# Linformer attention followed by a squared-ReLU FFN: a first batch in two token chunks, a new load order, crossbar transposes of Q, and attention spread over the FFN

## The chip, the cores and the metric

One core of one Trainium2 chip. The metric is device time in microseconds (us); medians of several runs are given. Engines: PE is the matrix engine, DVE the vector engine, ACT the scalar engine, POOL and SP the two engines that issue the DMAs here. PSUM is the memory that holds the accumulators of the matmuls. The granted clock is the share of full speed that PE's clock is allowed at a time, as the profile records it. All runs used are fast (executions without the slower clock that some show).

## The reference

Eight batches of 1024 tokens, 8 heads of 64. Keys and values are first projected along the sequence to 64 rows (E and F); the result of attention is the input of an FFN with 2048 hidden units.

```python
k_proj = np.einsum('ks,bhsd->bhkd', E, k)             # E, F: 64 x 1024
v_proj = np.einsum('ks,bhsd->bhkd', F, v)
scores = q @ k_proj.transpose(0, 1, 3, 2) / 8         # then softmax over 64 columns
x = (softmax(scores) @ v_proj)                        # -> (8192 tokens, 512)
h = np.maximum(x @ w_in, 0.0)                         # w_in 512 x 2048
out = (h * h) @ w_out                                 # w_out 2048 x 512
```

## The kernel before

Attention of a batch is a list of stages; the stages of batch b+1 are put between the FFN groups of batch b. Only PE's order is fixed by the program text; a scheduler orders the other engines. Batch 0's attention has no FFN to hide behind.

```python
kvq = load(0)                       # K, V, Q of batch 0, 1 MB each in bf16, cast while loading
...                                 # w_in in 4 pieces, w_out in 4 pieces; then load(1) in the loop
    def transpose_q(self, pr):      # one head pair: 8 PE transposes of 128x128
        ps = att_psum([P, 2, TCH], BF16)
        ...
        nc.vector.tensor_copy(t[:], ps[:])
    def scores(self, pr):           # 4 matmuls, then ACT: Exp over 128x1024
    def values(self, pr):           # sums (ones), values; ACT: Ln, Exp(-x); DVE: multiply
    def stages(self):               # (stage, FFN groups to wait before it)
        yield self.project, 3
        yield lambda: self.transpose_q(0), 2
        yield self.transpose_k, 1
        for pr in range(NPAIR):
            yield lambda pr=pr: self.scores(pr), 2
            if pr + 1 < NPAIR:
                yield lambda pr=pr: self.transpose_q(pr + 1), 1
            yield lambda pr=pr: self.values(pr), 2
...
        for stage_fn, _ in cur.stages():      # batch 0: everything before its FFN
            stage_fn()
        for b in range(B):
            nxt = Attention(b + 1, load(b + 1)) if b + 1 < B else None
            ...                               # FFN groups of b with the stages of b+1 between
```

An FFN group is 4 matmuls (first layer, one of 16 blocks, then ACT ReLU and DVE square) or 16 matmuls (second layer, one of 4 token blocks, then ACT copy and a store), for each half of the tokens: 40 groups, 256 matmuls of 128x512 per batch.

The softmax here doesn't subtract the row's maximum and nothing guards it: scores larger than these inputs give would overflow.

Of the kernel before, what the change touches and what calls it, by code (L numbers as in the profile page):

```python
# [13 lines left out]
PE = mybir.EngineType.PE  # L14


@with_exitstack
def kernel(
# [18 lines left out]
    assert D == 64 and KP == 64 and C == CM == 512 and S == 1024 and H % 2 == 0  # L37
# [5 lines left out]
    TCH = NT * P  # L43
    WP = 4
    SCALE = 1.0 / float(D) ** 0.5

# [5 lines left out]
    stage = ctx.enter_context(tc.tile_pool(name="stage", bufs=2))  # L52
# [11 lines left out]
    def att_psum(shape, dtype):  # L64
        return aps.tile(shape, dtype, tag="att", name="ps_att")

    def ffn_psum():
        return fps.tile([P, 512], F32, tag="ffn", name="ps_ffn")

    def load(b):  # L70
        tiles = []
        for name, src in (("K_sb", k), ("V_sb", v), ("Q_sb", q)):
            t = qkv_pool.tile([P, H, NI * D], BF16, name=name)
            nc.gpsimd.dma_start(t[:], src[b].rearrange("h (p i) d -> p h (i d)", i=NI))
            tiles.append(t)
        return tiles
# [3 lines left out]
    for src in (E, F):  # L80
        t = stage.tile([KP, S], F32, name="e_f32")
        nc.sync.dma_start(t[:], src[:])
        e_f32.append(t)
    kvq = load(0)
    nc.scalar.preload_act_table_set("natural_log_exp_and_others")
    ident = const_pool.tile([P, P], BF16, name="ident")
    make_identity(nc, ident[:])
    ones = const_pool.tile([P, D], BF16, name="ones")
# [5 lines left out]
    fw = FF // WP  # L94
    for j in range(WP):
        t = wpool.tile([P, NCB, fw], BF16, name=f"w_in_{j}")
        nc.gpsimd.dma_start(t[:], w_in_view[:, :, j * fw:(j + 1) * fw])
        w_in_sb.append(t)
    for j in range(WP):
        n = NFB // WP  # L100
        t = wpool.tile([P, n, DM], BF16, name=f"w_out_{j}")
        nc.gpsimd.dma_start(t[:], w_out_view[:, j * n:(j + 1) * n, :])
        w_out_sb.append(t)

    def w_in_blk(cb, fb):
        n = fw // P
        return w_in_sb[fb // n][:, cb, (fb % n) * P:(fb % n + 1) * P]

    def w_out_blk(fb):
        n = NFB // WP  # L110
        return w_out_sb[fb // n][:, fb % n, :]

    projT = []
    for n, src in zip(("ET", "FT"), e_f32):
        e_bf = stage.tile([KP, S], BF16, name="e_bf")
        nc.vector.tensor_copy(e_bf[:], src[:])
        ps = att_psum([P, NI, KP], BF16)
        view = e_bf[:].rearrange("k (p i) -> k i p", i=NI)
        for i in range(NI):
            nc.tensor.transpose(ps[:, i, :], view[:, i, :], ident[0:KP, 0:KP])  # L120
        t = const_pool.tile([P, NI, KP], BF16, name=n)
        nc.vector.tensor_copy(t[:], ps[:])
        projT.append(t)
    ET, FT = projT

    class Attention:


        def __init__(self, b, kvq):
            self.K, self.V, self.Q = kvq  # L130
            self.xT = x_pool.tile([P, NCB, 2 * TCH], BF16, name="xT")
            self.exp, self.ps_x = {}, {}

        def project(self):
            ps = att_psum([P, C], F32)
            kv = self.K[:].rearrange("p h (i d) -> p h i d", i=NI)
            vv = self.V[:].rearrange("p h (i d) -> p h i d", i=NI)
            for i in range(NI):
                f, l = i == 0, i == NI - 1
                nc.tensor.matmul(ps[0:KP, :], lhsT=ET[:, i, :], rhs=kv[:, :, i, :], start=f, stop=l)  # L140
                nc.tensor.matmul(ps[KP:P, :], lhsT=FT[:, i, :], rhs=vv[:, :, i, :], start=f, stop=l)  # L141

            self.kp = proj_pool.tile([KP, H, 2, D], BF16, name="kp")
            ps_k = ps[0:KP, :].rearrange("k (h d) -> k h d", h=H)
            nc.vector.tensor_copy(self.kp[:, :, 0, :], ps_k)
            nc.vector.tensor_copy(self.kp[:, :, 1, :], ps_k)
            self.vp = proj_pool.tile([P, H, D], BF16, name="vp")
            ps_v = ps[KP:P, :].rearrange("k (h d) -> k h d", h=H)
            nc.scalar.copy(self.vp[KP:P], ps_v)
            nc.scalar.copy(self.vp[0:KP], ps_v)  # L150

        def transpose_k(self):
            ps = att_psum([P, H, KP], BF16)
# [4 lines left out]
            self.kT = proj_pool.tile([P, H, KP], BF16, name="kT")  # L158
            nc.vector.tensor_copy(self.kT[:], ps[:])

        def transpose_q(self, pr):
            ps = att_psum([P, 2, TCH], BF16)
            for a in range(2):
                for n in range(NT):
                    nc.tensor.transpose(  # L165
                        ps[:, a, n * P:(n + 1) * P], self.Q[:, 2 * pr + a, n * P:(n + 1) * P], ident[:]
                    )
            t = qt_pool.tile([P, 2, TCH], BF16, name="qT")
            nc.vector.tensor_copy(t[:], ps[:])  # L169
            self.qt = getattr(self, "qt", {})  # L170
            self.qt[pr] = t

        def qT(self, h):
            return self.qt[h // 2][:, h % 2, :]


        def scores(self, pr):
            h0, h1 = 2 * pr, 2 * pr + 1
            ps = att_psum([P, 2, TCH], F32)
            lo, hi = slice(0, 64), slice(64, 128)  # L180
            q0, q1 = self.qT(h0), self.qT(h1)

            for o, bank, h, r, qt in ((lo, 0, h0, lo, q0), (hi, 0, h0, hi, q0),
                                      (hi, 1, h1, lo, q1), (lo, 1, h1, hi, q1)):
                nc.tensor.matmul(ps[o, bank, :], lhsT=self.kT[r, h, :], rhs=qt[r], start=True, stop=True)  # L185
            e = soft_pool.tile([P, 2, TCH], BF16, name="expT")
            nc.scalar.activation(e[:], ps[:], AF.Exp, scale=SCALE)  # L187
            self.exp[pr] = e

        def values(self, pr):  # L190
            h0, h1 = 2 * pr, 2 * pr + 1
            e = self.exp.pop(pr)
            lo, hi = slice(0, 64), slice(64, 128)

            quads = ((lo, 0, h0, lo, 0), (hi, 0, h1, hi, 1), (hi, 1, h1, lo, 1), (lo, 1, h0, hi, 0))
            ps_s = att_psum([P, 2, TCH], F32)
            for o, par, h, r, bank in quads:
                nc.tensor.matmul(ps_s[o, par, :], lhsT=ones[r, :], rhs=e[r, bank, :], start=True, stop=True)  # L198
            ps_x = att_psum([P, 2, TCH], F32)
            for o, par, h, r, bank in quads:  # L200
                nc.tensor.matmul(ps_x[o, par, :], lhsT=self.vp[r, h, :], rhs=e[r, bank, :], start=True, stop=True)  # L201
            rs = soft_pool.tile([P, 2, TCH], F32, name="rs")
            nc.scalar.activation(rs[:], ps_s[:], AF.Ln)  # L203
            nc.scalar.activation(rs[:], rs[:], AF.Exp, scale=-1.0)  # L204
            nc.vector.tensor_tensor(  # L205
                out=self.xT[:, pr, :].rearrange("p (a t) -> p a t", a=2), in0=ps_x[:], in1=rs[:], op=ALU.mult
            )

        def stages(self):

            yield self.project, 3
            yield lambda: self.transpose_q(0), 2
            yield self.transpose_k, 1
            for pr in range(NPAIR):
                yield lambda pr=pr: self.scores(pr), 2
                if pr + 1 < NPAIR:
                    yield lambda pr=pr: self.transpose_q(pr + 1), 1
                yield lambda pr=pr: self.values(pr), 2

    def ffn_groups(b, xT):  # L220

        groups = []

        def first(ch, hsq, fb):
            ps = ffn_psum()
            for cb in range(NCB):
                nc.tensor.matmul(  # L227
                    ps[:], lhsT=w_in_blk(cb, fb), rhs=xT[:, cb, ch * TCH:(ch + 1) * TCH],
                    start=(cb == 0), stop=(cb == NCB - 1),
                )  # L230
            r = relu_pool.tile([P, TCH], BF16, name="h_relu")
            nc.scalar.activation(r[:], ps[:], AF.Relu)  # L232
            nc.vector.tensor_tensor(out=hsq[:, fb, :], in0=r[:], in1=r[:], op=ALU.mult)  # L233

        def second(ch, hsq, tb):
            ps = ffn_psum()
            for fb in range(NFB):
                nc.tensor.matmul(  # L238
                    ps[:], lhsT=hsq[:, fb, tb * P:(tb + 1) * P], rhs=w_out_blk(fb),
                    start=(fb == 0), stop=(fb == NFB - 1),  # L240
                )
            o = out_pool.tile([P, DM], F32, name="o_sb")
            nc.scalar.copy(o[:], ps[:])  # L243
            nc.sync.dma_start(out_rows[b, 2 * tb + ch, :, :], o[:])

        for ch in range(2):
            hsq = hsq_pool.tile([P, NFB, TCH], BF16, name="hsq")
            for fb in range(NFB):
                groups.append(lambda ch=ch, hsq=hsq, fb=fb: first(ch, hsq, fb))
            for tb in range(NT):  # L250
                groups.append(lambda ch=ch, hsq=hsq, tb=tb: second(ch, hsq, tb))
        return groups

    with tc.manual_schedule(engines={PE}):
        cur = Attention(0, kvq)
        for stage_fn, _ in cur.stages():
            stage_fn()
        for b in range(B):
            nxt = Attention(b + 1, load(b + 1)) if b + 1 < B else None
# [41 lines left out]
```

## Time and profile before

| | before |
|---|---|
| time, median | 565.35 us (565.28 with the run beside the changed kernel) |
| span of the profiled run | 563.9 us |
| first FFN matmul | 41.23 us |
| batch 1's FFN begins | 117.55 us |
| period of the later batches | 64.42 us |

From the page of the kernel before: the first line is the busy time of each engine; then the span in 40 slices of 14.1 us with the busy tenths of PE, the granted PE clock in tenths of full speed, and the DMA engines' busy tenths; the last is the chain of work that ended last, by engine.

```profile
PE 522.4 (93%) x2841; PEld 232.1 (41%) x2896; DVE 178.8 (32%) x349; ACT 284.0 (50%) x433; POOL 28.4 (5%) x38
...
PE   1565999999999999999999999999999999999996
...
PEclk9856999999999999999999999999999999999999
DMA  8999996037431736019241546010101001020201
...
PE 79%; DMA 8%; ACT 7%; DVE 4%; issue 1%; POOL 1%; ACTq 0%; POOLq 0%
```

PE is the limit everywhere but in the first four slices. There the DMA engines are full, PE is idle for a good part, and its granted clock falls to 0.5 and 0.6 in the third and fourth slice.

The PE timeline of the kernel before: start, length, engine, source line, operation, destination <- sources, count, and in brackets the idle time before it with what ended it.

```profile
22.57 0.62 PE L165 MATMUL ps_att<-ident,Q_sb 128*128 128x128 bf16 x8 [1.48 <-DMA Q_sb<-in_q_dram]
...
35.12 1.01 PE L165 MATMUL ps_att<-ident,Q_sb 128*128 128x128 bf16 x8 [1.36 <-ACT expT L187]
...
41.23 1.06 PE L227 MATMUL ps_ffn<-xT,w_in_112 128*128 128x512 bf16 x2 [0.33 <-issue]
43.95 4.00 PE L227 MATMUL ps_ffn<-xT,w_in_112 128*128 128x512 bf16 x9 [1.65 <-DVE xT L205]
47.93 0.64 PE L140 MATMUL ps_att<-K_sb,ET 128*64 128x512 bf16 x1
53.04 0.58 PE L141 MATMUL ps_att<-V_sb,FT 128*64 128x512 bf16 x1 [4.48 <-DMA V_sb<-in_v_dram]
...
117.55 2.75 PE L227 MATMUL ps_ffn<-xT,w_in_112 128*128 128x512 bf16 x12
...
134.95 0.61 PE L165 MATMUL ps_att<-ident,Q_sb 128*128 128x128 bf16 x8 [0.31 <-DVE xT L205]
...
181.97 2.75 PE L227 MATMUL ps_ffn<-xT,w_in_112 128*128 128x512 bf16 x12
...
504.08 3.62 PE L227 MATMUL ps_ffn<-xT,w_in_112 128*128 128x512 bf16 x16
```

Read three things here. Batch 0's head pairs follow one another some 4.7 us apart until 41 us, because PE waits for ACT in each (the 35.12 line). PE then stops 4.48 us for V of batch 1, which the program asks for after only three FFN groups (the 53.04 line). And in steady state a Q transpose group can wait, too (the 134.95 line). From 181.97 - 117.55 comes the period, the time from the start of one batch's FFN to the next one's, of 64.42 us. Of it 256 x 0.216 = 55.3 us are FFN matmuls, which follow each other every 0.216 us here, and the other 9.1 us are attention with the waits around it. The last line shown is the start of the last batch.

### The profile page before, as it was taken

What the parts mean: (1) busy time and instruction counts of PE and PEld (TensorE: products, weight loads), DVE (VectorE), ACT (ScalarE), POOL (GpSimd) and SP (SyncE); (2) the same over time, 40 slices, a digit from 0 to 9 for tenths busy, and PEclk for the clock granted to TensorE, in tenths of its full rate; (3) what the DMA queues carried; (4) which work ended last, traced back from release to release, by engine and by line L of the source; (5) the groups of instructions that cost most, each with busy time, mean ns of one, the idle gap of its engine ahead of it and who ended that gap; (6) DMA issues with size and microseconds to landing.
All of it is one profiled execution on the core that took longest, in us unless ns stands there. A gap on an engine that the chain in (4) does not pass through costs nothing.

```text
span 563.9 us, 7122 instructions
## 1 busy us (share of the span) xinstructions
PE 522.4 (93%) x2841; PEld 232.1 (41%) x2896; DVE 178.8 (32%) x349; ACT 284.0 (50%) x433; POOL 28.4 (5%) x38
## 2 busy tenths in 40 slices
PE   1565999999999999999999999999999999999996
PEld 0221444444444444444444444444444444444442
DVE  1231524235050532325150442415141341504030
ACT  0261747347381656438282565628383564725351
POOL 6120100010000100010000100000000000000000
PEclk9856999999999999999999999999999999999999
DMA  8999996037431736019241546010101001020201
GB/s 152 207 206 207 207 212 115 33 67 126 92 58 58 128 78 112 20 60 146 71 81 56 100 88 132 2 75 1 56 20 38 38 7 69 0 76 0 76 0 74
DMA packets 38592, 47.11 MB, mean 84 GB/s; under 512 B 1568, under 2 KB 30240, under 8 KB 38560
## 3 DMA queue, kind: packets, MB, share of 16 engines
q0 software_dynamic: 29184, 29.36, 32.8%
q1 hardware_dynamic: 9376, 17.31, 8.2%
q8 instruction: 22, 0.36, 0.3%
q14 instruction: 10, 0.08, 0.0%
HBM read 59.24 MB, written 16.78 MB: 135 GB/s over the span
## 4 chain that ended last, share of the span: by engine, by line
PE 79%; DMA 8%; ACT 7%; DVE 4%; issue 1%; POOL 1%; ACTq 0%; POOLq 0%
PE ps_ffn L238 39%; PE ps_ffn L227 32%; DMA V_sb<-in_v_dram 4%; DMA w_in_114<-in_moe_w_in_dram 4%; DVE xT L205 3%; ACT rs L204 3%; PE ps_att L165 2%; ACT rs L203 2%; PE ps_att L140 2%; ACT h_relu L232 1%; PE ps_att L198 1%; PE ps_att L185 1%; DVE hsq L233 1%; PE ps_att L141 1%; PE ps_att L201 1%
## 5 line engine op out<-in xcount | busy, mean ns | idle before, releaser
L232 ACT ACTIVATE h_relu<-ps_ffn 128x512 bf16<-128x512 f32 x256 | 147.4, 597 | 73.1 <-PE ps_ffn L227 73.0
L233 DVE TENSOR_TENSOR hsq<-h_relu 128x512 bf16<-128x512 bf16 x256 | 105.4, 423 | 216.2 <-ACT h_relu L232 215.7
L238 PEld LDWEIGHTS <-hsq 128*128 128x128 bf16 x1024 | 98.8, 98 | 120.3 <-issue 4.5
L243 ACT COPY o_sb<-ps_ffn 128x512 f32<-128x512 f32 x64 | 37.5, 586 | 173.7 <-PE ps_ffn L238 173.7
L227 PE MATMUL ps_ffn<-xT,w_in_112 128*128 128x512 bf16 x255 | 64.7, 394 | 2.0 <-DVE xT L205 1.7
L238 PE MATMUL ps_ffn<-w_out_124,hsq 128*128 128x512 bf16 x255 | 65.6, 379 | 0.1
L238 PE MATMUL ps_ffn<-w_out_120,hsq 128*128 128x512 bf16 x255 | 65.6, 380 | 0.0
L238 PE MATMUL ps_ffn<-w_out_122,hsq 128*128 128x512 bf16 x248 | 65.1, 379 | 0.4
L238 PE MATMUL ps_ffn<-w_out_126,hsq 128*128 128x512 bf16 x235 | 62.3, 379 | 1.1
L227 PE MATMUL ps_ffn<-xT,w_in_114 128*128 128x512 bf16 x241 | 59.7, 381 | 1.5 <-issue 1.1
L227 PE MATMUL ps_ffn<-xT,w_in_116 128*128 128x512 bf16 x256 | 60.3, 380 | 0.0
L227 PE MATMUL ps_ffn<-xT,w_in_118 128*128 128x512 bf16 x248 | 58.6, 379 | 1.2 <-issue 1.1
L205 DVE TENSOR_TENSOR xT<-ps_att,rs 128x1024 bf16<-128x1024 f32 x32 | 39.2, 1225 | 53.0 <-ACT rs L204 53.0
L169 DVE COPY qT<-ps_att 128x1024 bf16<-128x1024 bf16 x32 | 22.1, 692 | 67.2 <-PE ps_att L165 67.0
L227 PEld LDWEIGHTS <-w_in_112 128*128 128x128 bf16 x256 | 23.8, 100 | 37.1 <-issue 13.5
L227 PEld LDWEIGHTS <-w_in_118 128*128 128x128 bf16 x256 | 24.2, 98 | 28.5 <-issue 1.6
L227 PEld LDWEIGHTS <-w_in_116 128*128 128x128 bf16 x256 | 23.6, 98 | 29.8 <-issue 4.5
L227 PEld LDWEIGHTS <-w_in_114 128*128 128x128 bf16 x256 | 23.8, 98 | 29.0 <-issue 3.9
L203 ACT ACTIVATE rs<-ps_att 128x1024 f32<-128x1024 f32 x32 | 32.9, 1027 | 4.9 <-PE ps_att L198 4.9
L204 ACT ACTIVATE rs<-rs 128x1024 f32<-128x1024 f32 x32 | 33.8, 1056 | 1.0
L187 ACT ACTIVATE expT<-ps_att 128x1024 bf16<-128x1024 f32 x32 | 32.7, 1023 | 1.9 <-PE ps_att L185 1.9
L141 PE MATMUL ps_att<-V_sb,FT 128*64 128x512 bf16 x64 | 18.6, 443 | 8.9 <-DMA V_sb<-in_v_dram 8.9
(43 smaller groups left out, 191.3 us busy)
## 6 DMA issues: line engine op xcount, KB each, us to landing
out_dram<-o_sb SPq DMA_DIRECT2D x64, 256.0 KB, 2.0
K_sb<-in_k_dram POOLq DMA_DIRECT2D x8, 1024.0 KB, 10.5
V_sb<-in_v_dram POOLq DMA_DIRECT2D x8, 1024.0 KB, 14.6
Q_sb<-in_q_dram POOLq DMA_DIRECT2D x8, 1024.0 KB, 10.9
w_in_112<-in_moe_w_in_dram POOLq DMA_DIRECT2D x1, 512.0 KB, 20.9
w_in_114<-in_moe_w_in_dram POOLq DMA_DIRECT2D x1, 512.0 KB, 22.0
w_in_116<-in_moe_w_in_dram POOLq DMA_DIRECT2D x1, 512.0 KB, 23.5
w_in_118<-in_moe_w_in_dram POOLq DMA_DIRECT2D x1, 512.0 KB, 25.3
```

The source lines that it names most:

```text
L140: nc.tensor.matmul(ps[0:KP, :], lhsT=ET[:, i, :], rhs=kv[:, :, i, :], start=f, stop=l)
L141: nc.tensor.matmul(ps[KP:P, :], lhsT=FT[:, i, :], rhs=vv[:, :, i, :], start=f, stop=l)
L169: nc.vector.tensor_copy(t[:], ps[:])
L187: nc.scalar.activation(e[:], ps[:], AF.Exp, scale=SCALE)
L203: nc.scalar.activation(rs[:], ps_s[:], AF.Ln)
L204: nc.scalar.activation(rs[:], rs[:], AF.Exp, scale=-1.0)
L205: nc.vector.tensor_tensor(out=self.xT[:, pr, :].rearrange("p (a t) -> p a t", a=2), in0=ps_x[:], in1=rs[:], op=ALU.mult)
L227: nc.tensor.matmul(ps[:], lhsT=w_in_blk(cb, fb), rhs=xT[:, cb, ch * TCH:(ch + 1) * TCH], start=(cb == 0), stop=(cb == NCB - 1),)
L232: nc.scalar.activation(r[:], ps[:], AF.Relu)
L233: nc.vector.tensor_tensor(out=hsq[:, fb, :], in0=r[:], in1=r[:], op=ALU.mult)
L238: nc.tensor.matmul(ps[:], lhsT=hsq[:, fb, tb * P:(tb + 1) * P], rhs=w_out_blk(fb), start=(fb == 0), stop=(fb == NFB - 1),)
L243: nc.scalar.copy(o[:], ps[:])
```

## The change

Its intent: let the FFN start sooner, keep PE from waiting at the start, and take the Q transposes off PE.

1. Batch 0 goes through attention in two halves of 512 tokens. Only the first half precedes the FFN, as two groups of two head pairs; the second half's attention lies between FFN steps of the first half.
2. Loads: K, then half of Q, then V in two pieces, the weights, and the other half of Q last. In the first chunk the FFN uses them as they come: four accumulators side by side for the first four blocks, contraction block by contraction block, then two token blocks at a time through the pieces of w_out.
3. Batch 1's attention starts at step 36 of 64 of batch 0.
4. From batch 2 on Q is transposed by one transposing DMA (`dma_start_transpose`, called the crossbar below), in place of 32 PE transposes and four DVE copies.
5. The second layer is cut into steps of 4 matmuls, and attention stages stand at fixed steps. One of the two copies of the projected V moves from ACT to DVE.

```diff
-    kvq = load(0)
+    load(K0[:], tokens(k, 0))
+    load(Q0[:, :, 0:4, :], tokens(q, 0, i=slice(0, 4)))
+    for g in range(2):
+        load(V0[:, 4 * g:4 * g + 4], tokens(v, 0, h=slice(4 * g, 4 * g + 4)))
 ...                                   # w_in, w_out in four pieces each, as before
+    load(Q0[:, :, 4:8, :], tokens(q, 0, i=slice(4, 8)))
 ...
+        def keep_v(self, ps_v, h=slice(0, 8)):
+            nc.scalar.copy(self.vp[HI, h], view)
+            nc.vector.tensor_copy(self.vp[LO, h], view)
+        def transpose_q_dma(self):
+            nc.sync.dma_start_transpose(
+                self.qT[:].rearrange("p h n t -> p (h n) t"), self.Q[:].rearrange("p h i d -> p (h i d)"))
 ...
-        for stage_fn, _ in cur.stages():
-            stage_fn()
+        att.project_k()
+        for hg in range(2):
+            att.transpose_q_chunk(0, Q0, hg)
+        att.transpose_k()
+        att.chunk_scores(0, 0)
+        att.chunk_scores(0, 1)
+        att.project_v(0)
+        att.chunk_sums(0, 0)
+        att.chunk_sums(0, 1)
+        att.project_v(1)
+        att.chunk_values(0, 0)
+        att.chunk_values(0, 1)
         for b in range(B):
+            if b == 0:
+                at(19, lambda: cur.transpose_q_chunk(1, Q0, 0))   # ... second chunk at steps 19 to 29
+            if b + 1 < B:
+                t0 = 36 if b == 0 else 4
+                at(t0, nxt.project)
+                at(t0 + 3, nxt.transpose_k)
+                if b == 0:                                        # four PE transpose groups for batch 1
+                    at(t0 + 5 + gap * pr, lambda pr=pr, a=nxt: a.transpose_q(pr))
+                else:
+                    nxt.transpose_q_dma()
+                    ...
+                at(t0 + 7 + gap * pr, lambda pr=pr, a=nxt: a.scores(pr))
+                at(t0 + 10 + gap * pr, lambda pr=pr, a=nxt: a.values(pr))
```

## The prediction

> **What bounds the kernel now.** The matrix engine: the page has PE busy 93% of the 563.9 us span, and 79% of the chain that ended last is PE. The timeline shows two regimes.
>
> *Steady state, from 117.6 us on.* Batches start 64.42 us apart (117.55, 181.97, 246.39 us). FFN matmuls follow each other every 0.216 us, 256 of them 55.4 us; the other 9.07 us are attention of the next batch, of which four Q transpose groups take 4 x 0.445 us, plus a 0.31 us wait. Windows by stage show PE 98 to 99% busy at full clock: only removed PE work helps.
>
> *Start, to 117.6 us.* One batch of FFN and two of attention, 55.4 + 2 x 9 = 73.5 us of warm PE work; 44 us are lost. K lands at 12.5, V 17.5, Q 22.6 us, 5.05 us per loaded MB; the DMA engines stay full until about 83 us. The four head pairs of batch 0 pass one after another, 4.7 us each (exp 1.02, Ln 1.03, Exp 1.06 on ACT, multiply 1.23 on DVE); FFN begins at 41.2 us, really at 44. PE then waits 4.5 us for V of batch 1 (to 53). The granted clock is 0.50 to 0.73 from 20 to 60 us; matmuls then follow every 0.427 us.
>
> **What changes.**
> 1. Half of Q goes before V, all weights before batch 1. Estimated arrivals from 5.05 us per MB: K 12.5, Q half 15 to 16.5, V by 21, w_in 23 to 31, w_out by 41, other Q half 44, K and V of batch 1 48 and 53.
> 2. Only half the tokens pass attention before the FFN, as two groups instead of four pairs. Estimated chain: K projection to 16, keeps and transposes to 19.4, scores and exps to 22, two Ln, two Exp, V keeps and multiplies to 30. The FFN begins at about 28.5 us instead of 41.2, its first 4 to 5 us at half clock (2 us lost). The Trainium skill, "TensorE: Matmul & The Clock Gate", Part 1, says about 3.4 us of activity releases the throttle; this trace agrees roughly (dense from 53.0, full rate near 57.5).
> 3. The second half's attention (3.6 us of PE) and batch 1's (8.8 us) fall between FFN groups, spaced wider than their ACT chains. Batch 1 should start at 28.5 + 2 + 55.4 + 3.6 + 8.8, about 98.5 instead of 117.6: 19 us won.
> 4. For batches 2 to 7, crossbar transposes replace 32 PE transposes and four 0.69 us DVE copies each. PE saves 2.1 us per batch, six times 12.5 us. The instruction order has them nearly a batch ahead. This trace has no transpose; the skill's "DMA: Bandwidth & Descriptors", Rules for kernel authors, states 261 GB/s, so 1 MB would take 4 us (estimate from that page). Even 10 us is hidden: the output has four buffers and stores come 3.5 us apart.
> 5. Attention spread: about 0.
>
> The end (4.5 us tail) stays.
>
> **Sum.** 565.35 - 19 - 12.5 = 534 us. Range 529 to 541 us. Chances: faster by over 2% 0.96, within 2% 0.02, slower 0.02.
>
> **What would show it.** First w_in matmul near 28.5 us; no PE wait on V of batch 1; full clock from 34 us; batch 1 starting near 98.5 us; period 62.3 us afterwards; transposes landing within 10 us and no PE wait on qT; PE busy about 96%.
>
> **What would make it wrong.** Transposes of tens of us that hold the output stores behind them, so that ACT and then PE wait; shorter Q runs slowing the first loads; the PSUM pool that FFN now shares with projection and transposes making PE wait; a clock low for longer, from PE pauses in the first FFN groups.

## The result, and the profile after

| | before | after |
|---|---|---|
| time, median | 565.28 us | 529.81 us |
| ratio | | 0.9373 (95% interval 0.9346 to 0.94) |
| span | 563.9 us | 527.9 us |
| first FFN matmul | 41.23 us | 26.74 us |
| batch 1's FFN begins | 117.55 us | 95.86 us |
| period, later batches | 64.42 us | 62.09 us |

A ratio is the mean time of one kernel's fast runs over that of the other's in the same rounds, so it is not quite the ratio of the medians.

From the page of the changed kernel, the same lines:

```profile
PE 504.0 (95%) x2693; PEld 219.8 (42%) x2744; DVE 170.6 (32%) x338; ACT 286.0 (54%) x426; POOL 29.6 (6%) x40
...
PE   1699999999999999999999999999999999999996
...
PEclk9989999999999999999999999999999999999999
DMA  9999999999965554282501932100102011010102
...
PE 94%; DMA 2%; ACT 1%; issue 1%; DVE 1%; POOLq 0%
```

From the DMA view of the changed kernel, the line of the crossbar transposes (issuing queue, count, median us from issue to landing), and from the view of the tile qT their spread:

```profile
qT<-Q_sb SPq DMA_TRANSPOSE x6, 9.0
...
DMA to landing us min/median/max: 5.5/9.0/16.1
```

PE is now full from the third slice on, and 94% of the chain is PE. Its timeline:

```profile
12.15 3.57 PE L177 MATMUL ps_bank<-K_sb,ET 128*64 128x512 bf16 x8 [4.62 <-DMA K_sb<-in_k_dram]
15.66 1.54 PE L203 MATMUL ps_bank<-ident,Q_sb 128*128 128x128 bf16 x16
...
22.52 0.41 PE L238 MATMUL ps_att<-expT,vp 64*64 64x256 bf16 x8
26.17 0.41 PE L238 MATMUL ps_att<-expT,vp 64*64 64x256 bf16 x8 [3.24 <-DVE vp L163]
26.74 5.09 PE L306 MATMUL ps_bank<-xT,w_in_110 128*128 128x512 bf16 x15 [0.16 <-issue]
31.87 3.61 PE L306 MATMUL ps_bank<-xT,w_in_112 128*128 128x512 bf16 x16
...
95.86 3.69 PE L306 MATMUL ps_bank<-xT,w_in_110 128*128 128x512 bf16 x16
...
158.02 3.62 PE L306 MATMUL ps_bank<-xT,w_in_110 128*128 128x512 bf16 x15
...
220.10 3.62 PE L306 MATMUL ps_bank<-xT,w_in_110 128*128 128x512 bf16 x16
...
468.44 3.62 PE L306 MATMUL ps_bank<-xT,w_in_110 128*128 128x512 bf16 x16
```

The lines at 26.74 and 31.87 us show the clock: the first 16 matmuls of the FFN (15 are recorded) took 5.1 us, the next 16 took 3.6 us. The single records of the first 16 follow each other every 0.427 us (half speed) until 30.3 us and every 0.216 us (full speed) after it; the clock record has 0.50 from 26.93 to 30.34 us. The wait of PE before 26.17 us is new; it comes back below.

Where the 36.0 us of span came from, as differences of the batch starts:

- the start: 117.55 - 95.86 = 21.7 us;
- six periods, 386.53 us before (504.08 - 117.55) and 372.58 after (468.44 - 95.86): 13.95 us;
- the last batch with its tail: 0.4 us.

### The profile page after: what moved, and what is told of

The parts are those of the page before. It is cut to its first block, busy times and chain, and to the rows that moved or that the text cites. A ratio compares the mean times of both kernels' runs of the same rounds, so it can differ in the third digit from the quotient of the medians.

```text
span 527.9 us, 6755 instructions
## 1 busy us (share of the span) xinstructions
PE 504.0 (95%) x2693; PEld 219.8 (42%) x2744; DVE 170.6 (32%) x338; ACT 286.0 (54%) x426; POOL 29.6 (6%) x40
## 4 chain that ended last, share of the span: by engine, by line
PE 94%; DMA 2%; ACT 1%; issue 1%; DVE 1%; POOLq 0%
PE ps_bank L312 42%; PE ps_bank L306 42%; PE ps_bank L169 2%; DMA K_sb<-in_k_dram 2%; PE ps_att L228 2%; PE ps_att L234 2%; PE ps_att L238 1%; PE ps_bank L177 1%; PE ps_bank L193 0%; ACT rs L247 0%; ACT rs L248 0%; PE ps_bank L213 0%; ACT h_relu L302 0%; DVE qT L207 0%; PE ps_bank L203 0%
## 5 line engine op out<-in xcount | busy, mean ns | idle before, releaser
L302 ACT ACTIVATE h_relu<-ps_bank 128x512 bf16<-128x512 f32 x256 | 149.7, 596 | 73.4 <-PE ps_bank L306 70.7
L312 PEld LDWEIGHTS <-hsq 128*128 128x128 bf16 x1024 | 96.6, 98 | 122.7 <-issue 12.2
L319 ACT COPY o_sb<-ps_bank 128x512 f32<-128x512 f32 x64 | 37.4, 585 | 117.5 <-PE ps_bank L312 114.6
L263 DVE TENSOR_TENSOR xT<-ps_att,rs 128x1024 bf16<-128x1024 f32 x28 | 34.3, 1225 | 105.9 <-ACT rs L248 105.9
L312 PE MATMUL ps_bank<-w_out_122,hsq 128*128 128x512 bf16 x250 | 64.6, 379 | 0.7 <-issue 0.5
L312 PE MATMUL ps_bank<-w_out_124,hsq 128*128 128x512 bf16 x252 | 64.7, 379 | 0.5 <-issue 0.5
L312 PE MATMUL ps_bank<-w_out_120,hsq 128*128 128x512 bf16 x247 | 64.2, 380 | 0.8 <-issue 0.3
L312 PE MATMUL ps_bank<-w_out_118,hsq 128*128 128x512 bf16 x250 | 64.7, 379 | 0.2
L306 PE MATMUL ps_bank<-xT,w_in_110 128*128 128x512 bf16 x249 | 58.8, 387 | 0.7 <-issue 0.5
L306 PE MATMUL ps_bank<-xT,w_in_114 128*128 128x512 bf16 x252 | 58.9, 379 | 0.3
L306 PE MATMUL ps_bank<-xT,w_in_112 128*128 128x512 bf16 x248 | 58.4, 380 | 0.4
L306 PE MATMUL ps_bank<-xT,w_in_116 128*128 128x512 bf16 x249 | 58.0, 379 | 0.5 <-issue 0.3
L247 ACT ACTIVATE rs<-ps_att 128x1024 f32<-128x1024 f32 x32 | 32.7, 1024 | 12.5 <-PE ps_att L234 12.4
L306 PEld LDWEIGHTS <-w_in_110 128*128 128x128 bf16 x256 | 24.9, 99 | 32.6 <-issue 5.0
L306 PEld LDWEIGHTS <-w_in_116 128*128 128x128 bf16 x256 | 24.5, 98 | 31.4 <-issue 2.9
L306 PEld LDWEIGHTS <-w_in_114 128*128 128x128 bf16 x256 | 24.4, 98 | 29.9 <-issue 1.6
L306 PEld LDWEIGHTS <-w_in_112 128*128 128x128 bf16 x256 | 23.9, 98 | 30.3 <-issue 3.2
L238 PE MATMUL ps_att<-expT,vp 64*64 64x512 bf16 (+1 forms) x144 | 12.5, 355 | 3.3 <-DVE vp L163 3.2
L76 POOL DMA_DIRECT2D K_sb<-in_k_dram x8 | 7.1, 891 | 131.8 <-PE ps_bank L170 127.3
## 6 DMA issues: line engine op xcount, KB each, us to landing
V_sb<-in_v_dram POOLq DMA_DIRECT2D x7, 1024.0 KB, 22.9
```

What stands on the lines that cost most here:

```text
L238: nc.tensor.matmul(ps[o, par], lhsT=self.vp[r, 2 * pr + a, :], rhs=e[r, par], start=True, stop=True)
L247: nc.scalar.activation(rs[:], ps[:], AF.Ln)
L263: nc.vector.tensor_tensor(out=self.xT[:, pr].rearrange("p c a t -> p a c t"), in0=ps_x[:].rearrange("p a (c t) -> p a c t", c=2), in1=rs[: ...
L302: nc.scalar.activation(r[:], ps[:], AF.Relu)
L306: nc.tensor.matmul(ps[:], lhsT=w_in_blk(cb, fb), rhs=self.xT[:, cb, c].rearrange("p a t -> p (a t)"), start=(cb == 0), stop=(cb == NCB - 1),)
L312: nc.tensor.matmul(ps[:], lhsT=self.hsq[c][:, fb, tb * P:(tb + 1) * P], rhs=w_out_blk(fb), start=(fb == 0), stop=(fb == NFB - 1),)
```

## The experiments

Twelve runs followed, of ten new kernels (e0 is the changed kernel again, e6b is e6 again), all with correct results. Batch starts come from each run's PE timeline.

### Steady state: the crossbar, or the spread?

**e2_before_xbar.** The kernel before; only Q of batches 2 to 7 goes through the crossbar, other stages keep their places.

```diff
+            if b >= 2:
+                self.qTb = qt_pool.tile([P, H, NT, P], BF16, name="qTb")
+                nc.sync.dma_start_transpose(self.qTb[:]..., self.Q[:]...)
 # stages(): no transpose_q for b >= 2, its waits added to the next stage
```

> The kernel before with one thing taken from the change: Q of batches 2 to 7 is transposed by the crossbar, all other attention groups keep their places. Theory A, crossbar: period from batch 1 to 7 falls from 64.42 by 1.8 to 2.1 us, six times, time 553 to 554.5 us. Theory B, spread: the matrix engine's time comes back as waits in the old places, period above 63.5 us, time above 560 us.

Measured: 551.73 us, ratio 0.9773 (0.9753 to 0.9793). Period 62.17 instead of 64.42: 2.25 us per batch, more than the 1.8 to 2.1 us that theory A named. From its PE timeline, two starts of a batch's FFN:

```profile
240.72 2.75 PE L241 MATMUL ps_ffn<-xT,w_in 128*128 128x512 bf16 x12
...
302.89 2.75 PE L241 MATMUL ps_ffn<-xT,w_in 128*128 128x512 bf16 x12
```

**e1_pe_q_all.** The changed kernel with PE transposes in every batch.

```diff
-                if b == 0:
-                    for pr in range(NPAIR):
-                        at(t0 + 5 + gap * pr, lambda pr=pr, a=nxt: a.transpose_q(pr))
-                else:
-                    nxt.transpose_q_dma()
+                for pr in range(NPAIR):
+                    at(t0 + 5 + gap * pr, lambda pr=pr, a=nxt: a.transpose_q(pr))
```

> The changed kernel with the Q transposes of every batch back on the matrix engine (eight 128x128 transposes and one DVE copy per head pair, spread as the change spreads those of batch 1). Theory A, crossbar: the matrix engine's 4 x 0.445 us per batch were what the crossbar removed, so the period from batch 1 on rises from 62.09 to about 63.9 us, and the time from 529.8 to about 540.5 us; the rest of the 2.33 us that the period fell by (about 0.55 us) is the spread and stays. Theory B, spread: most of the gain per batch came from the new places of the attention groups; then the period stays below 62.6 us and the time below 533 us.

Measured: 541.01 us, ratio 0.957 (0.9547 to 0.9592). Period 63.87: 1.78 us over 62.09, which is 4 x 0.445. From its PE timeline:

```profile
222.38 3.62 PE L306 MATMUL ps_bank<-xT,w_in 128*128 128x512 bf16 x16
...
286.25 3.62 PE L306 MATMUL ps_bank<-xT,w_in 128*128 128x512 bf16 x16
```

What follows: theory A holds in both directions. The two parts share a piece. The spread (with the smaller rearrangements that came with it) alone saves 64.42 - 63.87 = 0.55 us per batch, but once the crossbar is there it saves only 62.17 - 62.09 = 0.08. So of the 2.25 us that the crossbar saves in the old places, 1.78 is PE work, and the other 0.47 goes with the transpose groups in their old places; the spread removes it, too. Of this 0.47 us the trace of the kernel before shows 0.31 as a wait of PE (L165 for DVE, once in each batch), which neither e2 nor e1 has. The remaining 0.16 us stands in no list of waits and stays open.

**e7_xbar_twice.** The changed kernel with each crossbar transpose done twice.

```diff
                     nxt.transpose_q_dma()
+                    nxt.transpose_q_dma()
```

> The changed kernel with every crossbar transpose done twice into the same tile (12 instead of 6, the second waits for the first). If the transposes are hidden, as predicted for up to 10 us each: within 1 us of the changed kernel (529 to 531 us), period from batch 2 on 62.1 us. If they are near the critical path, through the output stores behind them on the same queue or through the data engines: over 3 us slower, with waits of ACT on output buffers or of the matrix engine on qT.

Measured: 529.81 us, ratio 0.938 (0.9366 to 0.9394), period 62.08 or 62.09 from batch 2 on. The transposes are off the critical path at this place in the kernel, doubled or not. They took up to 24.9 us to land, and PE waits for none of them:

```profile
DMA to landing us min/median/max: 5.5/5.6/24.9
```

### The start: projection later, chunks, loads

**e5_before_late_proj.** The kernel before; in batch 0 only, the stages of batch 1 begin after 12 FFN groups instead of 3.

```diff
-            wait = pending[0][1] if pending else 0
+            wait = (12 if b == 0 else pending[0][1]) if pending else 0
```

> The kernel before with one thing changed: in batch 0 the projection of batch 1 comes after FFN group 12 instead of group 3, the later groups keep their distances. Theory D, late projection: the 4.5 us wait for V of batch 1 goes, and the clock, which this pause held at half, rises about 5 us sooner, so 6 to 7 us faster: 558.5 to 559.5 us. Theory C, chunks: the start is set by batch 0's attention chain, and some of the wait was filled anyway or comes back at the end of batch 0, where attention now ends later: 562 us or more.

Measured: 559.28 us, ratio 0.99 (0.9883 to 0.9917). Batch 1 at 111.57 instead of 117.55 us: 6.0 us (5.4 by the medians of the call, 564.66 and 559.28). The wait for V of batch 1 is gone, and the clock record is at 1.00 from 50.13 us on, instead of 58.83. So theory D is true for 6 us of the 21.7, not for more.

```profile
111.57 2.75 PE L227 MATMUL ps_ffn<-xT,w_in 128*128 128x512 bf16 x12
```

**e3_whole_batch0.** The changed kernel with batch 0 not cut; Q is loaded whole, second.

```diff
-    load(Q0[:, :, 0:4, :], tokens(q, 0, i=slice(0, 4)))
+    load(Q0[:], tokens(q, 0))
-    load(Q0[:, :, 4:8, :], tokens(q, 0, i=slice(4, 8)))
-        att.chunk_scores(0, 0) ...            # and the second chunk at steps 19 to 29
+        att.scores(0); att.transpose_q(1); att.project_v(0); att.project_v(1); att.values(0); ...
```

> The changed kernel with batch 0 not cut: all of Q is loaded second, all four head pairs of batch 0 pass attention before its FFN, nothing of batch 0's attention is left to the FFN. Theory C, chunks: the ACT and DVE chain of four pairs of about 4 us each ends near 39 us, the FFN begins about 12 us later than at 26.7 us, and 3.6 us of attention leave the FFN: about 8.5 us slower than the changed kernel, 538 us. Theory D, later projection and warm clock: the start was won mainly because the matrix engine no longer waits for V of batch 1 and stays at full clock; then the cost is under 4 us, below 534 us.

Measured: 537.09 us, ratio 0.9493 (0.9472 to 0.9514). FFN from 37.72 us, batch 1 at 103.81: 7.95 us later than in the changed kernel. In this trace K came 1.2 us later than there (13.35 against 12.15 us), so about 1 us of that is not the cut's. Theory C holds.

```profile
103.81 3.69 PE L305 MATMUL ps_bank<-xT,w_in 128*128 128x512 bf16 x16
```

**e4_old_loads.** The changed kernel, two chunks, but K, V, Q whole in the old order.

```diff
-    load(Q0[:, :, 0:4, :], tokens(q, 0, i=slice(0, 4)))
-    for g in range(2):
-        load(V0[:, 4 * g:4 * g + 4], tokens(v, 0, h=slice(4 * g, 4 * g + 4)))
+    load(V0[:], tokens(v, 0))
+    load(Q0[:], tokens(q, 0))
-    load(Q0[:, :, 4:8, :], tokens(q, 0, i=slice(4, 8)))
```

> The changed kernel with the loads of batch 0 in the old order (K, V, Q whole, then weights), attention still in two chunks. If the order of loads matters: the first Q transposes wait for Q at 22.3 us instead of running at 15.7 us, the chain and the FFN start about 5 to 6 us later (near 32 us), time about 535 us, and w_in may be waited for a little. If the chain on ACT and DVE alone set the start: within 1.5 us of the changed kernel, 530 to 531 us.

Measured: 537.77 us, ratio 0.9511 (0.9492 to 0.953). FFN from 34.76 us, batch 1 at 104.64: 8.8 us later. The longest waits of PE in this run (total us, times, longest):

```profile
PE ps_bank L201 <- DMA Q_sb<-in_q_dram: 6.6, 1, 6.6
...
PE ps_bank L175 <- DMA K_sb<-in_k_dram: 4.8, 1, 4.8
PE ps_att L236 <- DVE vp L161: 3.0, 1, 3.0
```

and the start of batch 1:

```profile
104.64 3.69 PE L304 MATMUL ps_bank<-xT,w_in 128*128 128x512 bf16 x16
```

The FFN began 8.0 us later, where 5 to 6 were expected. Q at 22.51 instead of 15.66 us is already 6.85 us of it. The other 1.17 us lie in the chain from the transposes to the FFN, 12.25 us instead of 11.08. The clock is a likely part of that: after the pause it is recorded at 0.50 from 19.23 to 29.47 us, where the changed kernel has 1.00, and the 16 transposes took 1.89 us instead of 1.54. The profiled run was the slowest of the four, with the lowest mean clock (0.984, the others 0.997); by the medians the old order costs 8.0 us, not 8.8.

**e9_whole_old_loads.** Both undone at once.

> The changed kernel with both parts of the new start undone: batch 0 not cut and K, V, Q loaded whole in the old order; late projection, spread and crossbar stay. Undone alone, the cut cost 7.3 us and the load order 8.0 us. If the two add up, because the one moves the start of batch 0's attention chain and the other shortens it: about 545 us, batch 1 near 111 to 112 us, as in the kernel before with only the late projection (111.57). If they cover each other: 538 to 541 us.

Measured: 541.53 us, ratio 0.9583 (0.957 to 0.9596); FFN from 41.73 us, batch 1 at 107.83:

```profile
107.83 3.69 PE L304 MATMUL ps_bank<-xT,w_in 128*128 128x512 bf16 x16
```

My sum of 545 us failed. The two together are worth 107.83 - 95.86 = 12.0 us. Added to the old loads, the cut alone brings 107.83 - 104.64 = 3.2 us. Added to the whole batch, the new load order alone brings 107.83 - 103.81 = 4.0 us (about 5 but for the late K of that run). So 4 to 5 us exist only with both. (By the ratios times 565 us it is 11.9 together, 4.1 and 5.1 alone, so that about 3 us are left; two runs of the changed kernel, below, differ by 1.2 us.) A reason that the traces show for part of it: half a batch needs only half of Q, at 15.66 us, while a whole batch in the new order waits until 18.43 us for all of it. The clock differs as well: the FFN begins with 4.5 us at half clock in e3 and e9, and with 3.4 us in the changed kernel. How the rest divides was not measured.

Along one path, then, the 21.7 us of the start are 6.0 (later projection, e5), 12.0 (cut and load order together, e9 to the changed kernel), and 111.57 - 107.83 = 3.7 us between e5 and e9. That last part holds the contraction-block order of the first FFN groups, the V copies split between ACT and DVE, and the new stage positions; in e5 PE still waits 1.65 us for the last multiply inside the first FFN groups, in e9 it does not. The FFN begins at the same time in both (41.76 and 41.73 us), so all of the 3.7 us lie after its start. About 1 us more is the clock, an estimate: it is recorded at 1.00 from 50.13 us in e5 and from 46.28 in e9, some 16 and 11 matmuls at 0.427 us instead of 0.216. The rest was not taken apart.

### The wait that the change brought

**e6_v_keep_dve.** In the changed kernel one copy of the projected V is on ACT; for the second group it stood behind two Ln and two Exp (ACT at 25.29 us), and PE waited 3.24 us for it. Here both copies of batch 0 are on DVE.

```diff
+            if self.b == 0:
+                nc.vector.tensor_copy(self.vp[HI, h], view)
+            else:
+                nc.scalar.copy(self.vp[HI, h], view)
-            nc.scalar.copy(self.vp[HI, h], view)
```

> The changed kernel with both copies of batch 0's projected V on DVE (ACT made one of them, and the second V group's copy stood behind two Ln and two Exp; the matrix engine waited 3.24 us for it before the last values matmuls). If that wait set the start of the FFN: first w_in matmul near 25.0 us instead of 26.7, and if the clock stays high through the shorter pause, up to 2 us more: 526.5 to 528.3 us. If the multiplies on DVE or the Exp on ACT set it anyway: within 0.5 us of 529.8.

Measured: 528.29 us, ratio 0.935 (0.9325 to 0.9374), against 0.9373 of the changed kernel from other rounds: too close to tell. So both were run again together, on one chip.

**e0_after**, the changed kernel again:

> The changed kernel itself, unedited, as the yardstick for the other runs of this call: 529.8 us, ratio to before 0.9375. Both theories of the other runs expect the same here.

Measured: 531.01 us, ratio 0.9396 (0.9383 to 0.9409).

**e6b_v_keep_dve**, the same kernel as e6:

> The same kernel as the one with both V copies of batch 0 on DVE, again, beside the changed kernel on one chip. Its first trace had the FFN start 0.97 us and batch 1 1.62 us sooner than the changed kernel's. If that is the removed wait for the V copy plus a clock that now stays high: 1 to 2 us faster than the changed kernel of this call. If it was run to run variation of the clock: within 0.5 us.

Measured: 528.82 us, ratio 0.9358 (0.9345 to 0.9371): 2.2 us faster than e0_after, and the intervals do not touch. Between e6 and the first run of the changed kernel it was 1.5 us. Its PE timeline:

```profile
22.50 0.41 PE L241 MATMUL ps_att<-expT,vp 64*64 64x256 bf16 x8
23.53 0.41 PE L241 MATMUL ps_att<-expT,vp 64*64 64x256 bf16 x8 [0.62 <-DVE vp L166]
24.67 14.17 PE L309 MATMUL ps_bank<-xT,w_in 128*128 128x512 bf16 x62 [0.73 <-DVE xT L292]
...
42.98 0.62 PE L206 MATMUL ps_bank<-ident,Q_sb 128*128 128x128 bf16 x8 [1.55 <-DMA Q_sb<-in_q_dram]
```

The wait before the last values matmuls fell from 3.24 to 0.62 us. The FFN starts sooner, and its first 64 matmuls take 14.0 us at full clock from the beginning (24.67 to 38.68) instead of 15.5 (26.74 to 42.22). Then PE meets the next limit: it waits 1.55 us for the second half of Q.

How much of the gain is the wait, and how much the clock, is not settled by this. e1 starts with the same program as the changed kernel and waits as long, yet its FFN runs at full speed at once (13.8 us for the first 64 matmuls), and its batch 1 begins at 94.57 us, only 0.5 us after that of e6b (94.03):

```profile
25.98 0.41 PE L238 MATMUL ps_att<-expT,vp 64*64 64x256 bf16 x8 [3.24 <-DVE vp L163]
26.55 13.96 PE L306 MATMUL ps_bank<-xT,w_in 128*128 128x512 bf16 x62 [0.16 <-issue]
```

The traces of e0 and e7, with the same wait, show half clock for 3.41 us after it, as that of the changed kernel does. So the wait was followed by the slower clock in three of four traces, not in all: batch starts of single traces differ by 1.7 us (94.57 to 96.24) for this one program.

**e10_later_chunk1.** The wait for the second half of Q taken away as well: the second chunk's transposes two steps later, the rest of its stages one step later.

```diff
-                at(19, lambda: cur.transpose_q_chunk(1, Q0, 0))
-                at(20, lambda: cur.transpose_q_chunk(1, Q0, 1))
-                at(22, lambda: cur.chunk_scores(1, 0))          # ... to 29
+                at(21, lambda: cur.transpose_q_chunk(1, Q0, 0))
+                at(22, lambda: cur.transpose_q_chunk(1, Q0, 1))
+                at(23, lambda: cur.chunk_scores(1, 0))          # ... to 30
```

> The kernel with both V copies on DVE, and the second chunk's Q transposes two FFN steps later, its scores, sums and values one step later. There the FFN began at 24.67 us and the matrix engine then waited 1.55 us for the second half of Q (landed near 43 us). If that wait is all that stands there: 1.5 us faster than that kernel, 527.3 us, ratio to before about 0.933. If the shift only turns it into a wait for the second chunk's multiplies before its FFN: within 0.5 us of that kernel, ratio 0.935 to 0.937.

Measured: 527.13 us, ratio 0.9322 (0.9309 to 0.9335), batch 1 at 93.22 us. No wait for Q is left in its trace. This is the fastest version that ran; it ran on another chip than e6b, so their ratios to the kernel before are to be compared (0.9322 and 0.9358, whose intervals do not touch), not their times.

**e8_xbar_batch1.** On top of e6: batch 1's Q, too, by the crossbar.

```diff
-                if b == 0:
-                    ...                       # PE transposes for batch 1
-                else:
-                    nxt.transpose_q_dma()
+                nxt.transpose_q_dma()
```

> The kernel with V copies on DVE, and batch 1's Q too transposed by the crossbar instead of the matrix engine. Q of batch 1 lands near 58 us, the first scores of batch 1 come near 70 us, while the data engines are full until about 90 us. If the transpose lands within 10 us: another 1.8 us (4 x 0.445) gone, about 526.5 us. If the full data engines delay it beyond 70 us: the matrix engine waits on qT near 70 us, and the time stays at 528 us or rises.

Measured: 539.74 us, ratio 0.9553 (0.954 to 0.9566): 10.9 us slower than e6b. Its waits of PE (one line), and its SP timeline (the first transpose is batch 1's, the last one ran when the DMA engines had room):

```profile
PE ps_att L231 <- DMA qT<-Q_sb: 9.9, 1, 9.9
```

```profile
59.41 19.11 SPq L223 DMA_TRANSPOSE qT<-Q_sb  x1
...
322.78 4.14 SPq L223 DMA_TRANSPOSE qT<-Q_sb  x1
```

The same 1 MB transpose held its queue 19.11 us at 59 us, with the DMA engines full of loads, and 4.14 us later. PE reached the scores of batch 1 some 11.6 us after the transpose was issued and stood 9.9 us for it; after that pause the clock is recorded at 0.50 from 74.43 to 84.67 us. A slow transpose alone does no harm: e7 has one that held its queue for 21.45 us, at 127.56 us, also with the DMA engines nearly full, and PE did not wait: it is batch 4's, whose scores come after 220 us. That the crossbar is hidden in the changed kernel is therefore a matter of when: it keeps PE transposes for the one batch whose Q is needed soon and while the loads are still running.

## Why the prediction was right or wrong

The time was inside the range, at its lower edge (529.81; 529 to 541 with 534 named). The mechanisms were right; two terms of the sum were too small.

- *Term "19 us won" at the start: it was 21.7.* The named pieces against the trace: FFN start 28.5 against 26.74 us; half-clock loss 2 against 1.66 (42.22 - 26.74 - 64 x 0.216); second chunk's attention 3.6 against 3.58; batch 1's attention 8.8 against 8.59. The start of the FFN is the mis-sized piece: the scores began at 18.62 us where the estimated chain has 19.4, the exponentials ended at 21.03 instead of 22, and the last multiply ended at 27.93 instead of 30. The clock was up for most of that chain: the K projection ran at half speed throughout, ten of the 16 transposes after it still came every 0.107 us, and from 16.7 us on they came every 0.056. The Trainium skill's "TensorE: Matmul & The Clock Gate", Part 1, puts the release at about 3.4 us of sustained activity. Here it came later: 4.5 us after the first matmul of the K projection (12.15 to 16.69), and in the kernel before 5.8 us after the pause for V (53.04 to 58.83). The same section says that the window of observation is free-running, which would allow this; no run here tests it.
- *Term "12.5 us" in steady state: it was 14.0.* 2.09 us per batch should have been 2.33. The PE work was right (1.78 by e1); of what goes with the transpose groups I had counted one wait of 0.31 us, while e2 shows 0.47 beyond the PE work, and 0.08 more comes from the spread.
- *"Attention spread: about 0".* True beside the crossbar (0.08 us per batch), but only because the crossbar takes most of what the spread would save; without it the spread brings 0.55 (e1).
- *"Even 10 us is hidden".* Right for time (e7). But "landing within 10 us" was wrong: from 5.5 to 16.1 us, median 9.0. The estimate of 4 us came from 261 GB/s, which "DMA: Bandwidth & Descriptors" gives from one kernel (in the section Latency and other measured facts; the prediction named another section). The shortest transpose here held its queue for 3.93 us and landed 5.5 us after issue. The three slower ones, at 77, 104 and 127 us (6.9 to 13.2 us on the queue), ran while the DMA engines were full.
- *Item 1 named "all weights before batch 1" as a change.* It was so before. The wait for V of batch 1 went because its use moved to step 36, as item 3 said; e5 measured that at 6.0 us.
- *Half-length Q runs as a risk.* It did not come: the POOL queue's waits for landing ended at 12.39 (K), 15.06 (half Q, 512-byte writes) and 17.62 us (half V, 1024-byte writes), 2.67 and 2.56 us apart. The skill's "DMA: Bandwidth & Descriptors", Specifications, gives 512 bytes as the least run for full rate; this agrees.
- *Not foreseen:* the 3.24 us wait for a V copy behind ACT's Ln and Exp, worth 1.5 to 2.2 us by the two comparisons (e6, e6b); how much of that is the clock is open. It hid some of the first miss: in the trace of e6b, without it, the start is won by 23.5 us (117.55 - 94.03).

## What to carry to other kernels

When a kernel is bound by one engine in steady state, price a removed instruction by its spacing there plus the waits around it (here 0.445 us for a group of eight transposes), and expect two cures of the same wait to share its gain. At the start, look for what each stage really needs: cutting the data and reordering its loads brought 12 us together, and 3 to 5 us alone. A DMA that replaces engine work is free only where it lands before its result is needed. DMA engines that were nearly full cost nothing in e7, where the result was needed late, and 9.9 us of waiting in e8, where it was needed 11.6 us after issue. So test it at the place where it runs. And compare single traces of a start with care: one program gave batch starts 1.7 us apart here, with the state of the clock.

## What the Trainium skill lacked or had wrong

- "DMA: Bandwidth & Descriptors", Latency and other measured facts: 261 GB/s for a DMA transpose with a non-contiguous middle dimension, but no figure beside other traffic. Here 1 MB at best held its queue for 3.93 us (about 267 GB/s, an estimate from 1.05 MB) and landed 5.5 us after issue; with the DMA engines full it landed after 16.1 us at worst in the changed kernel, 21.4 us in e8 and 24.9 us in e7.
- "TensorE: Matmul & The Clock Gate", Part 4: about 275 ns for a 128x128 PE transpose in one kernel, and that full clock does not engage for transposes. Here eight take 0.445 us of PE's time between FFN matmuls at full clock, 0.056 us each, and removing 32 brings 1.78 us (e1). The spacing is what counts; Part 4 does not give it, though Part 1 has the same 56 ns for matmuls of this width. Whether transposes alone would raise the clock no run here tests.
- The same page, Part 1, warns that clock records can be unreliable, without a number. In e5 the granted clock reads 1.00 up to 50 us, because the trace has no clock record before 50.13 us. Yet the transposes between 22.9 and 36.7 us follow each other every 0.107 us and the FFN matmuls from 44.9 to 49.9 us every 0.427 us, half the speed seen later. The kernel before runs at the same spacings where its record has 0.50 (24.70 to 48.59 us). The spacing of matmuls is the safer reading.
